# One more step between sign, product, pick, mask and turn of the weights in a top-k attention kernel

## The chip, the cores and the metric

The kernel runs on one core of one Trainium2 chip. The metric is the time of one execution on the device, in microseconds (us). Five runs of the kernel before gave a median of 993.47 us, from 991.87 to 994.64.

## The reference

The inputs are q, k and v of 8 batches, 8 heads, 576 positions and 64 features. Each row of scores keeps its 32 largest entries. The attention output, 4608 tokens of 512 features, then goes through a mixture of 8 experts, each of which takes at most 80 tokens. Shortened to what matters:

```python
scores = scale * np.matmul(q, k.transpose(0, 1, 3, 2))
kth = np.partition(scores, -32, axis=-1)[..., -32:-31]          # 32nd largest of each row
scores = np.where(scores >= kth, scores, -1e9)
attn = np.exp(scores - scores.max(-1, keepdims=True))
attn = attn / (attn.sum(-1, keepdims=True) + 1e-9)
x = np.matmul(attn, v)                                          # -> (4608, 512)
logits = x @ w_gate
expert_idx = np.argmax(logits, axis=1)                          # one expert of 8 for each token
...                                                             # of each expert's tokens the 80 with the largest gate
out[tok_idx] = gate_w[tok_idx, None] * (np.maximum(x[tok_idx] @ w1[e], 0.0) @ w2[e])
```

## The kernel before

The attention part fills some 855 of the 992 us. It works on pairs of heads, `n` = 0 to 31. A pair of heads has 9 *units*: 128 rows of scores against 576 columns each. Four row tiles `t` = 0 to 3 give two units, one for each head (`h` = 0 and 1); the last 64 rows of both heads share one unit (`h` = 2). That makes 288 units, numbered through.

What happens to a unit, and on which engine:

- **front** (L226, L233): TensorE (PE) multiplies q by k into the PSUM tile `sp`, of which there is one; ScalarE (ACT) copies it to the tile `s`. One front makes the scores of two units, or of the one tail unit. It is emitted four steps ahead of their search.
- **parts, search** (L241, L252, L260): VectorE (DVE) takes the 8 largest of six parts, and from these 48 candidates the 24 largest, eight at a time.
- **sign** (L257): ACT writes the sign of (24th largest minus score) and, by the accumulator, how many scores lie above.
- **product** (L263): GpSimd (POOL) multiplies scores and signs into `y`, which has two buffers.
- **max of y** (L265): DVE finds the next 8 candidates below the 24th in `y`.
- **pick** (L268): DVE picks the 32nd largest by the count, as the threshold `thr`.
- **mask** (`below`; L279 or L277): from scores and threshold, on POOL for units of even number and on ACT for odd ones.
- **turn of the weights** (`turn_w`; L315, L320, L322, L324): PE transposes scores and subtracts masks in PSUM, ACT takes the exponential into `wT`. One turn takes the two units of a row tile, or the tail unit.
- **back** (L335): PE multiplies `wT` by v; the row sums come out beside it. Then **over** (L347), the reciprocal on DVE, and **divide** (L358) on ACT, into `xn`.
- After the last row tile of a pair of heads **norm** follows (L367 to L391): store of `xn`, transposes (L201, L375), the gate's logits (L380, L387), and after every eighth pair of heads the gates (L402 to L425). **turn** (L201, L214) transposes q and k of the next pair.

The order is written out by hand, in `run`: under a manual schedule, `step(i)` emits one step of the loop over the units, and every engine works through its own part of that order strictly in sequence. In step i, DVE does the search of unit i and, by a string of letters, pieces of earlier units. The table `back` says by how many units earlier:

```python
back = dict(a=0, b=1, c=1, d=1, e=1, y=2, g=3, h=4, m=4, H=3, M=3)
for c in "GybGcGdGeGGzag" if i % 2 else "GGbghHmMyGcGdGeGza":
```

`G` is one of the six parts, `e` ends with the sign, `y` is the product, `g` the max of y, `h` and `H` are picks, `m` and `M` masks, `z` the reciprocal. Picks and masks come in even steps only, two units at a time. Then follow the turn of the weights of unit i - 4 (if a turn ends there), the divide, the front of unit i + 4, the back of unit i - 5, and in steps without a front the turn of q and k or a piece of norm.

So for each two steps POOL has this order: one mask, two products. DVE has: parts and search of two units, max of y, two more pieces, max of y, pick, pick.

All tiles of the loop come from pools whose buffers rotate: `s` has 5 (each of two units), sign 2, mask 3, the small tiles of the search 4. The three `vb` tiles hold v of three pairs of heads; the loads of q, k and v of pair n + 2 are issued by SyncE (SP) in the step of unit (t = 2, h = 1) of pair n.

After the attention comes the choice of tokens (`route`, DVE alone for the most part) and then the experts, on PE.

Of the kernel before, what the change touches and what calls it, by code (L numbers as in the profile page):

```python
# [9 lines left out]
F32 = mybir.dt.float32  # L10
BF16 = mybir.dt.bfloat16
# [16 lines left out]
def kernel(  # L28
# [12 lines left out]
    B, H, S, D = q.shape  # L41
# [8 lines left out]
    P = 128  # L50
    HP = H // 2
    NP = B * HP
# [11 lines left out]
    NU = NP * UPP  # L64
# [84 lines left out]
    class Attention:  # L149


        def __init__(self, stack, lean):
            self.lean = lean
            pool = lambda name, bufs, **kw: stack.enter_context(tc.tile_pool(name=name, bufs=bufs, **kw))
            self.nat, self.qkp, self.rows = pool("nat", 1), pool("qkp", 2), pool("rows", 2)
            self.small, vpool = pool("small", 4), pool("vpool", 1)
            self.ps_s, self.ps_w, self.ps_c = (pool(n, k, space=PSUM) for n, k in (("ps_s", 1), ("ps_w", 1), ("ps_c", 2)))
            self.qk, self.turned, self.lg = {}, {}, {}
            self.s, self.top, self.cnt, self.y, self.mask, self.w, self.xn = ({} for _ in range(7))
            self.thr, self.z = thr_all, z_all  # L160
            self.odd = set()


            self.vb = []
            for j in range(1 if lean else 3):
                t = vpool.tile([P, NK, 2, D + 1], F32, name=f"vb{j}")
                nc.gpsimd.memset(t[:, :, :, D : D + 1], 1.0)
                nc.gpsimd.memset(t[: P - TL, NF, :, :], 0.0)
                self.vb.append(t)

            self.xT = vpool.tile([P, NK * P], F32, name="xT")
            nc.gpsimd.memset(self.xT[:, S:], 0.0)

        def load(self, n, b, hp):
            one = bass.ds(b, 1)
            tiles = []
            for name, src in (("qn", q), ("kn", k)):
                t = self.nat.tile([P, NK, 2, D], F32, name=name, tag=name)
                for h in range(2):
                    nc.sync.dma_start(  # L180
                        t[:, 0:NF, h, :],
                        src[one, 2 * hp + h, : NF * P, :].rearrange("o (c p) d -> p (o c) d", p=P))
                nc.sync.dma_start(
                    t[0:TL, NF, :, :], src[one, 2 * hp : 2 * hp + 2, NF * P :, :].rearrange("o h p d -> p (o h) d"))
                tiles.append(t)
            t = self.vb[n % len(self.vb)]
            for h in range(2):
                nc.sync.dma_start(
                    t[:, :NF, h, :D], v[one, 2 * hp + h, : NF * P, :].rearrange("o (c p) d -> p (o c) d", p=P))
            nc.sync.dma_start(  # L190
                t[P - TL :, NF, :, :D], v[one, 2 * hp : 2 * hp + 2, NF * P :, :].rearrange("o h p d -> p (o h) d"))
            self.qk[n] = tiles

        def four(self):
            return self.ps_s.tile([P, 4, 512], F32, name="sp", tag="sp")
# [20 lines left out]
        def front(self, n, t):  # L216

            qT, kT = self.turned[n]
            m = P if t < NF else TL
            i = n * UPP + 2 * t  # L220
            ps = self.four()
            for j in range(2):
                for h in range(2):
                    d = slice(D * h, D * h + D)
                    o = ps[:, 2 * h + j, :HS] if t < NF else ps[TL * h : TL * h + TL, j, :HS]
                    nc.tensor.matmul(o, lhsT=qT[d, t * P : t * P + m], rhs=kT[d, j * HS : (j + 1) * HS], start=True, stop=True)  # L226
            g = 2 if t < NF else 1
            s = self.rows.tile([P, 2 * S], F32, name="s", tag="s", bufs=2 if self.lean else 5)
            for h in range(g):
                self.s[i + h] = s[:, h * S : (h + 1) * S]  # L230
            for j in range(0, 2 * g, 2 if i == 0 else 2 * g):
                w = 2 if i == 0 else 2 * g
                nc.scalar.activation(s[:, j * HS : (j + w) * HS].rearrange("p (j c) -> p j c", c=HS), ps[:, j : j + w, :HS],  # L233
                                     Act.Copy, scale=TINY)
# [10 lines left out]
        def search(self, i):  # L245

            s, cand = self.s[i], self.top[i]
            top = self.top[i] = self.small.tile([P, G0 // 8 - 1, 8], F32, name="top", tag="top")
            w9 = self.small.tile([P, 16], F32, name="w9", tag="w9")
            for r in range(G0 // 8):  # L250
                dst = top[:, r, :] if r < G0 // 8 - 1 else w9[:, :8]
                nc.vector.max(out=dst, in_=cand)  # L252
                if r == G0 // 8 - 1:

                    sign = self.rows.tile([P, S], BF16, name="sign", tag="sign")
                    cnt = self.small.tile([P, 1], F32, name="cnt", tag="cnt")
                    nc.scalar.activation(sign, s, Act.Sign, bias=w9[:, 7:8], scale=-1.0, accum_out=cnt)  # L257
                yield
                if r < G0 // 8 - 1:
                    nc.vector.match_replace(out=cand, in_to_replace=dst, in_values=cand, imm_value=LOW)  # L260
                    yield
            y = self.rows.tile([P, S], F32, name="y", tag="y")
            nc.gpsimd.tensor_tensor(out=y, in0=s, in1=sign, op=Alu.mult)  # L263
            yield
            nc.vector.max(out=w9[:, 8:], in_=y)  # L265
            yield
            pick = self.small.tile([P, TOP_K - G0 + 1], F32, name="pick", tag="pick")
            nc.vector.scalar_tensor_tensor(out=pick, in0=past, scalar=cnt, in1=w9[:, 7:], accum_out=self.thr[:, i : i + 1],  # L268
                                           op0=Alu.is_equal, op1=Alu.mult)
            yield  # L270

        def below(self, i):

            self.top.pop(i)
            self.mask[i] = self.rows.tile([P, S], BF16, name="mask", tag="mask", bufs=3)
            if i in self.odd:
                nc.scalar.activation(self.mask[i], self.s[i], Act.Relu, bias=self.thr[:, i : i + 1], scale=-1.0)  # L277
                return
            nc.gpsimd.tensor_scalar(self.mask[i], self.s[i], self.thr[:, i : i + 1], None, op0=Alu.is_lt)  # L279
# [147 lines left out]
        def run(self, slow):  # L427

            units = []
            for n in range(NP):  # L430
                for t in range(NF):
                    units += [(n, t, 0), (n, t, 1)]
                units.append((n, NF, 2))
            self.odd = set(range(1, NU, 2))
            first, second = {}, {}
            later = []
            due = []
            drawn = []
            ready = {}

            def whole(i):

                return 0 <= i < NU and units[i][2] > 0

            def step(i, last):
                if 0 <= i < NU:
                    n, t, h = units[i]
                    if t == 2 and h == 1 and n + 2 < NP:
                        self.load(n + 2, *divmod(n + 2, HP))
                    if t in (1, 3) and h == 0 and slow and n:  # L450
                        slow.pop(0)()
                    if t == 0 and h == 0 and n + 1 < NP:
                        due.append(n + 1)
                    first[i] = self.parts(i)


                back = dict(a=0, b=1, c=1, d=1, e=1, y=2, g=3, h=4, m=4, H=3, M=3)
                for c in "GybGcGdGeGGzag" if i % 2 else "GGbghHmMyGcGdGeGza":
                    if c == "G":
                        if 0 <= i < NU:  # L460
# [15 lines left out]
                drawn.clear()  # L476

                def back():
                    if whole(i - 5):
                        self.back(*units[i - 5][:2])  # L480
                        drawn.append(units[i - 5][:2])


                rest = whole(i - 4) and units[i - 4][2] == 2
                if rest:
                    back()
                if whole(i - 4):
                    self.turn_w(*units[i - 4][:2])
                for u in done:
                    self.divide(*u)  # L490

# [7 lines left out]
                if not rest:  # L499
                    back()  # L500
# [10 lines left out]
                for n, cs in ends:  # L511
                    b, hp = divmod(n, HP)
# [1 line left out]
                    ready[later[-1]] = 0  # L514

            with tc.manual_schedule():
                self.load(0, 0, 0)
                self.load(1, *divmod(1, HP))
                nc.sync.dma_start(wg, moe_w_gate.rearrange("(c p) e -> p c e", p=P))
                self.turn(0)  # L520
                i = -4
                while i < NU + 6 or later:
                    step(i, i >= NU + 5)
                    i += 1
            assert not slow and not due

        def batch(self, b):

            for hp in range(HP):
                self.load(hp, b, hp)  # L530
                self.turn(hp)
                for t in range(NK):
                    self.front(hp, t)
                    i = hp * UPP + 2 * t
# [380 lines left out]
```

## Time and profile before

| | |
|---|---|
| median of 5 runs | 993.47 us (991.87 to 994.64) |
| the profiled execution | 993.92 us; span from its first to its last instruction 992.2 us |
| mean granted TensorE clock | 0.984 |
| from the first POOL mask to the last | 22.36 to 855.63 us |
| choice of tokens and experts | from about 867 us to the end |

| engine | busy us | share of the span |
|---|---|---|
| PE (matmul) | 879.8 | 89% |
| DVE | 804.6 | 81% |
| ACT | 799.2 | 81% |
| POOL | 627.2 | 63% |

How to read it: a group's line names the source line, the engine, the operation and the tiles, then the busy time and the mean of one in ns, then the idle time of the engine just before and what ended it. Matmul ends are modelled, so a busy PE need not be PE at its peak. In the view of the waits the columns are: who waited for whom, us in total, times, the longest in us. In the timeline: start in us, duration in us, engine, line, operation, out<-in, and in brackets the idle time before and what ended it. In the table of stages: the stage, its length, then busy us of PE, PEld (weight loads), DVE, ACT and POOL with the number of instructions in brackets, the granted clock, the DMA engines' share and GB/s.

### The profile page before, as it was taken

What the parts mean: (1) busy time and instruction counts of PE and PEld (TensorE: products, weight loads), DVE (VectorE), ACT (ScalarE), POOL (GpSimd) and SP (SyncE); (2) the same over time, 40 slices, a digit from 0 to 9 for tenths busy, and PEclk for the clock granted to TensorE, in tenths of its full rate; (3) what the DMA queues carried; (4) which work ended last, traced back from release to release, by engine and by line L of the source; (5) the groups of instructions that cost most, each with busy time, mean ns of one, the idle gap of its engine ahead of it and who ended that gap; (6) DMA issues with size and microseconds to landing.
All of it is one profiled execution on the core that took longest, in us unless ns stands there. A gap on an engine that the chain in (4) does not pass through costs nothing.

```text
span 992.2 us, 35679 instructions
## 1 busy us (share of the span) xinstructions
PE 879.8 (89%) x13368; PEld 708.2 (71%) x13368; DVE 804.6 (81%) x4928; ACT 799.2 (81%) x1652; POOL 627.2 (63%) x474
## 2 busy tenths in 40 slices
PE   5899999999989999999899999999899998689896
PEld 3677777777767777777677777777677776678896
DVE  5798989898989898999989898989898989471110
ACT  3899999999989999999899999999899999501110
POOL 3677767676767777777677676767677777402111
PEclk9999999999999999999999999999999999978998
DMA  3444453333323233333111222222222200084920
GB/s 72 101 124 132 127 135 92 92 92 92 93 66 79 79 88 86 88 92 93 42 44 42 47 50 50 51 50 49 49 50 50 49 14 14 16 338 155 376 71 27
DMA packets 167797, 85.76 MB, mean 86 GB/s; under 512 B 117696, under 2 KB 154560, under 8 KB 167616
## 3 DMA queue, kind: packets, MB, share of 16 engines
q1 hardware_dynamic: 166592, 80.78, 29.3%
q0 software_dynamic: 1024, 2.62, 0.9%
q8 instruction: 107, 1.75, 0.7%
q14 instruction: 74, 0.61, 0.2%
HBM read 63.19 MB, written 20.19 MB: 84 GB/s over the span
## 4 chain that ended last, share of the span: by engine, by line
DVE 38%; PE 25%; ACT 21%; POOL 9%; issue 6%; DMA 0%; POOLq 0%; ACTq 0%; DVEq 0%
DVE cand L241 11%; DVE w L265 10%; ACT sign L257 6%; POOL y L263 5%; PE cc L335 5%; ACT wT L324 4%; DVE cand L260 4%; DVE top L252 4%; PE sp L201 4%; POOL mask L279 4%; PE yp L799 4%; PE sp L226 4%; ACT s L233 4%; ACT mask L277 3%; DVE pick L268 3%
## 5 line engine op out<-in xcount | busy, mean ns | idle before, releaser
L241 DVE MAX8 cand<-s 128x8 f32<-128x96 f32 x1728 | 400.9, 246 | 9.3 <-ACT s L233 9.1
L263 POOL TENSOR_TENSOR y<-s,sign 128x576 f32<-128x576 f32 x288 | 365.3, 1280 | 66.4 <-ACT sign L257 66.4
L279 POOL TENSOR_SCALAR mask<-s,thr_all 128x576 bf16<-128x576 f32 x144 | 247.9, 1722 | 178.3 <-DVE pick L268 176.5
L335 PEld LDWEIGHTS cc<-vb,wT 128*64 128x64 f32 x5760 | 183.0, 139 | 114.0 <-ACT wT L324 100.5
L265 DVE MAX8 w<-y 128x8 f32<-128x576 f32 x288 | 216.4, 751 | 46.0 <-POOL y L263 46.0
L335 PE MATMUL cc<-vb,wT 128*64 128x65 f32 x5760 | 205.3, 226 | 42.8 <-ACT wT L324 42.8
L257 ACT ACTIVATE sign<-s,w 128x576 bf16<-128x576 f32 x288 | 225.0, 781 | 6.9 <-POOL y L263 1.9
L226 PE MATMUL sp<-both 64*128 64x288 f32 (+1 forms) x1280 | 203.4, 437 | 17.6 <-ACT part L387 9.6
L233 ACT ACTIVATE s<-sp 128x1152 f32<-128x1152 f32 (+1 forms) x161 | 167.4, 1041 | 12.3 <-PE sp L226 9.9
L315 PE MATMUL ab<-ident,s 128*128 128x128 f32 x1148 | 176.0, 282 | 0.0
L324 ACT ACTIVATE wT<-ab 128x1024 f32<-128x1024 f32 (+1 forms) x159 | 149.0, 937 | 0.0
L226 PEld LDWEIGHTS sp<-both 64*128 64x128 f32 (+1 forms) x1280 | 106.0, 180 | 56.6 <-ACT part L387 11.5
L315 PEld LDWEIGHTS ab<-ident,s 128*128 128x128 f32 x1148 | 127.9, 142 | 11.6 <-issue 0.9
L252 DVE MAX8 top<-cand 128x8 f32<-128x48 f32 x576 | 116.1, 202 | 4.5
L277 ACT ACTIVATE mask<-s,thr_all 128x576 bf16<-128x576 f32 x144 | 112.3, 780 | 6.9 <-DVE pick L268 6.5
L320 PEld LDWEIGHTS <-mask 128*128 128x128 bf16 x1440 | 94.0, 98 | 31.6 <-POOL mask L279 29.1
L260 DVE MATCH_REPLACE8 cand<-top,cand 128x48 f32<-128x48 f32 x576 | 111.0, 193 | 0.0
L358 ACT ACTIVATE xn<-cc,z_all 128x64 f32<-128x64 f32 (+1 forms) x320 | 86.7, 320 | 1.2 <-DVE z_all L347 0.8
L315 PE MATMUL cc<-ident,s 128*128 128x128 f32 x288 | 78.9, 274 | 0.0
L322 ACT ACTIVATE wT<-cc 128x256 f32<-128x256 f32 (+1 forms) x160 | 57.0, 356 | 16.5 <-PE cc L320 15.3
L268 DVE SCALAR_TENSOR_TENSOR pick<-past,cnt,w 128x9 f32<-128x9 f32 x288 | 60.4, 223 | 0.3 <-ACT xn L358 0.3
L257 ACT ACTIVATION_READ_ACCUMULATOR sign<-s,w 128x1 f32 x288 | 58.4, 203 | 0.0
(187 smaller groups left out, 905.9 us busy)
## 6 DMA issues: line engine op xcount, KB each, us to landing
w<-in_moe_w_dram SPq DMA_DIRECT2D x10, 2048.0 KB, 11.8
w<-in_moe_w_dram SPq DMA_DIRECT2D x24, 512.0 KB, 4.6
out_dram<-zero SPq DMA_DIRECT2D x9, 1024.0 KB, 6.5
qn<-in_q_dram SPq DMA_DIRECT2D x64, 128.0 KB, 2.6
kn<-in_k_dram SPq DMA_DIRECT2D x64, 128.0 KB, 2.6
vb<-in_v_dram SPq DMA_DIRECT2D x64, 128.0 KB, 2.7
xd<-xn SPq DMA_DIRECT2D x32, 256.0 KB, 3.9
qn<-in_q_dram SPq DMA_DIRECT2D x32, 32.0 KB, 2.5
```

The lines of the kernel that those rows point to most:

```text
L226: nc.tensor.matmul(o, lhsT=qT[d, t * P : t * P + m], rhs=kT[d, j * HS : (j + 1) * HS], start=True, stop=True)
L233: nc.scalar.activation(s[:, j * HS : (j + w) * HS].rearrange("p (j c) -> p j c", c=HS), ps[:, j : j + w, :HS], Act.Copy, scale=TINY)
L241: nc.vector.max(out=cand[:, j, :], in_=s[:, j * S // NG : (j + 1) * S // NG])
L252: nc.vector.max(out=dst, in_=cand)
L257: nc.scalar.activation(sign, s, Act.Sign, bias=w9[:, 7:8], scale=-1.0, accum_out=cnt)
L260: nc.vector.match_replace(out=cand, in_to_replace=dst, in_values=cand, imm_value=LOW)
L263: nc.gpsimd.tensor_tensor(out=y, in0=s, in1=sign, op=Alu.mult)
L265: nc.vector.max(out=w9[:, 8:], in_=y)
L279: nc.gpsimd.tensor_scalar(self.mask[i], self.s[i], self.thr[:, i : i + 1], None, op0=Alu.is_lt)
L315: nc.tensor.matmul(dst[h][c], lhsT=sc[:, keys[c]], rhs=ident, start=c == 0 or (c == NF and h == 0), stop=False, is_transpose=True, skip_gr ...
L324: nc.scalar.activation(wT[:, : g * NF, :], ab.rearrange("p h c r -> p (h c) r")[:, : g * NF, :], Act.Exp, scale=scale / TINY)
L335: nc.tensor.matmul(cc[r : r + TL, o], lhsT=wT[:, h * NF + c if c < NF else 2 * NF + h, r : r + TL], rhs=vb[:, c, h if t < NF else r // TL, ...
```

## The change

The distances in `back` grow: the product comes three steps after the unit's own step instead of two, the max of y four instead of three, the two picks and masks four and five instead of three and four. The turn of the weights goes from four steps behind to six, the back from five to seven; reciprocal and division stay in the step after the back. As picks and masks come in even steps only, the two units that share such a step are now an odd one (`h`, `m`) and the even one after it (`H`, `M`); before, they were an even one (`h`, `m`) and the odd one after it. The string of letters is the same, and so is which units' masks are made on POOL.

More buffers carry the longer lives: 7 for `s` instead of 5, 3 for sign instead of 2, 4 for mask instead of 3, 7 instead of 4 for the small tiles. The load of v is taken out of `load` and issued two units later. `batch`, a path for other data, loads v in a call of its own.

```diff
-            self.small, vpool = pool("small", 4), pool("vpool", 1)
+            self.small, vpool = pool("small", 7), pool("vpool", 1)
...
+            self.qk[n] = tiles
+
+        def load_v(self, n, b, hp):
+            one = bass.ds(b, 1)
             t = self.vb[n % len(self.vb)]
...
-            s = self.rows.tile([P, 2 * S], F32, name="s", tag="s", bufs=2 if self.lean else 5)
+            s = self.rows.tile([P, 2 * S], F32, name="s", tag="s", bufs=2 if self.lean else 7)
...
-                    sign = self.rows.tile([P, S], BF16, name="sign", tag="sign")
+                    sign = self.rows.tile([P, S], BF16, name="sign", tag="sign", bufs=3)
...
-            self.mask[i] = self.rows.tile([P, S], BF16, name="mask", tag="mask", bufs=3)
+            self.mask[i] = self.rows.tile([P, S], BF16, name="mask", tag="mask", bufs=4)
...
+            LT = 6
...
                     if t == 2 and h == 1 and n + 2 < NP:
                         self.load(n + 2, *divmod(n + 2, HP))
+                    if t == 3 and h == 1 and n + 2 < NP:
+                        self.load_v(n + 2, *divmod(n + 2, HP))
...
-                back = dict(a=0, b=1, c=1, d=1, e=1, y=2, g=3, h=4, m=4, H=3, M=3)
+                back = dict(a=0, b=1, c=1, d=1, e=1, y=3, g=4, h=5, m=5, H=4, M=4)
...
                 def back():
-                    if whole(i - 5):
-                        self.back(*units[i - 5][:2])
-                        drawn.append(units[i - 5][:2])
-                rest = whole(i - 4) and units[i - 4][2] == 2
+                    if whole(i - LT - 1):
+                        self.back(*units[i - LT - 1][:2])
+                        drawn.append(units[i - LT - 1][:2])
+                rest = whole(i - LT) and units[i - LT][2] == 2
                 if rest:
                     back()
-                if whole(i - 4):
-                    self.turn_w(*units[i - 4][:2])
+                if whole(i - LT):
+                    self.turn_w(*units[i - LT][:2])
...
-                while i < NU + 6 or later:
-                    step(i, i >= NU + 5)
+                while i < NU + LT + 3 or later:
+                    step(i, i >= NU + LT + 2)
```

## The prediction

> **What bounds the kernel now.** I read the waits of the whole run first. They say who waits, not what matters.
>
> ```profile
> POOL mask L279 <- DVE pick L268: 176.5, 143, 3.3
> ...
> POOL y L263 <- ACT sign L257: 66.4, 63, 12.3
> ...
> DVE w L265 <- POOL y L263: 46.0, 49, 2.8
> ...
> PEld L320 <- POOL mask L279: 29.1, 35, 2.3
> DVE z_all L347 <- PE cc L335: 27.2, 18, 4.5
> ...
> ACT both L214 <- PE sp L201: 23.1, 31, 2.1
> ```
>
> POOL waits for DVE (mask for pick), DVE for POOL (max of y), POOL for ACT (product for sign). Next I read POOL's timeline in mid-run, from mask to mask.
>
> ```profile
> 300.43 1.72 POOL L279 TENSOR_SCALAR mask<-s,thr_all 128x576 bf16<-128x576 f32 x1 [1.10 <-DVE pick L268]
> 302.12 2.52 POOL L263 TENSOR_TENSOR y<-s,sign 128x576 f32<-128x576 f32 x2
> 305.74 1.72 POOL L279 TENSOR_SCALAR mask<-s,thr_all 128x576 bf16<-128x576 f32 x1 [1.10 <-DVE pick L268]
> ...
> 312.74 1.28 POOL L263 TENSOR_TENSOR y<-s,sign 128x576 f32<-128x576 f32 x1
> 314.66 1.27 POOL L263 TENSOR_TENSOR y<-s,sign 128x576 f32<-128x576 f32 x1 [0.64 <-ACT sign L257]
> 317.03 1.72 POOL L279 TENSOR_SCALAR mask<-s,thr_all 128x576 bf16<-128x576 f32 x1 [1.10 <-DVE pick L268]
> ```
>
> One stretch (two units) lasts 5.31 us, the next but one 5.98, where the second product waits 0.64 for a sign. Counted over the run, from the mask at 38.09 to the last at 855.63 there are 141 stretches in 817.5 us, mean 5.80: 70 of 5.31, 62 above 5.9. DVE's timeline shows how a short one closes.
>
> ```profile
> 304.67 0.76 DVE L265 MAX8 w<-y 128x8 f32<-128x576 f32 x1
> 305.35 0.21 DVE L268 SCALAR_TENSOR_TENSOR pick<-past,cnt,w 128x9 f32<-128x9 f32 x1
> 305.48 0.08 DVE L268 DVE_READ_ACCUMULATOR pick<-past,cnt,w 128x1 f32 x1
> 305.54 0.23 DVE L268 SCALAR_TENSOR_TENSOR pick<-past,cnt,w 128x9 f32<-128x9 f32 x1
> 305.69 0.08 DVE L268 DVE_READ_ACCUMULATOR pick<-past,cnt,w 128x1 f32 x1
> ```
>
> It is a ring: mask 1.69 to the first product, the two products to 304.64, max of y from 304.67, first pick done at 305.56, mask at 305.74. Nothing in it is idle but hand-overs. That the ring binds, and not DVE's load, shows at the end, where DVE has little left to do and the stretch is as long (DVE 3.01 of 5.30):
>
> ```profile
> 317.03:368.78 51.75, 47.42 (x698) 37.63 (x695) 47.98 (x303) 48.95 (x102) 38.01 (x27) 1.00 0.34 88
> ...
> 850.33:855.63 5.30, 4.14 (x88) 3.86 (x84) 3.01 (x13) 3.64 (x10) 4.20 (x3) 1.00 0.01 3
> ```
>
> The first line is the repeating block, two pairs of heads, nine stretches: 51.75 us, of which nine rings are 47.8. ACT is busy 48.95, and of its 2.80 idle 2.35 end on PE: 1.28 before `both` (0.98 and 0.30), 0.20 xT, 0.10 part, 0.66 wT, 0.11 s. So two things bind: the ring in short stretches, ACT with PE in long ones.
>
> **Step 1, the waits for signs.** In the stretch at 305.74 the first product's sign was done 3.1 us before the product began, the second's 0.3 us (sign and accumulator end at 308.34, product at 308.66). That 0.3 is why only the second product waits. One step later (2.65 us, half a stretch), and with the units' parities exchanged, both have about 4 us. From 38.09 on these waits are 46.8 us; I take all of them away. Late next is what ACT itself needs, step 3.
>
> **Step 2, the ring gets a pick longer.** In the order of the changed kernel POOL's mask still belongs to the even unit, but that is now the second pick of the step; in the old order the mask waits for the first. The second accumulator is read 0.21 after the first (305.48, 305.69). Queued behind the mask are both products, and behind those DVE's two maxima, so it is paid in full: 5.31 + 0.21 = 5.52, times 141 is +30 us on the ring. Product to max and pick to mask keep their distances, so the ring isn't opened. Nine rings are 49.7.
>
> **Step 3, ACT.** Its work is the same. The waits for PE before `both`, xT and part stay, for ACT's order around them is the same: 48.95 + 1.58 = 50.5 a block. The waits before wT and s (0.77) I let go: the order puts the tail unit's turn and the logits, which share a step now, into different ones, and no turn waits for a mask of its own step (PE waited 52 us for masks; ACT hides most of it, so I count nothing more). Bounds: 49.7, the ring, if ACT's waits overlap; 51.3 if all 2.35 stay. I take 50.5: 1.25 less a block, 141/9 = 15.7 blocks, **-19.6 us**.
>
> **Step 4, the waits of POOL itself.** In the new order 286 products wait for two engines, an extra wait instruction each: the sign, and POOL's own third instruction back (the buffer of y), long done. Its price can be read from the masks: those that wait for one engine only stand 1.03 idle, the others 1.10.
>
> ```profile
> 22.36 1.74 POOL L279 TENSOR_SCALAR mask<-s,thr_all 128x576 bf16<-128x576 f32 x1 [1.03 <-DVE pick L268]
> ```
>
> So 0.07 when POOL waits for it, nothing while POOL works on the instruction ahead; products follow back to back and their signs are done, so I take 0. Bounds 0 to 0.2 each (0.16 from pick's end to mask, and 0.04 of overlap lost).
>
> The Trainium skill speaks against the change here: "Perfetto Trace Analysis", section Identifying Dependency Chains, says that an instruction that waits on several engines may get an extra semaphore instruction before it, and "Advanced Engine Details and Errata", section Network/Comms, puts reading a semaphore at 50 to 100 ns. By these, as an estimate, 286 products would pay 14 to 29 us, and the sum below would come to between -6 and +9 instead of -20.
>
> **Step 5, start, gates, end.** At the start DVE waits 2.83 and 1.12 us for products held by signs; bounds -6 to 0, I take -3. Three times the gates stretch three stretches by some 2.8 us together; that is DVE work and stays. At the end POOL makes y of the last unit after the last mask, not before it: mask to product 1.69, product 1.28, max to pick 0.68, pick and hand-over 0.39, ACT's mask 0.7 comes before the exponential that began 2.11 after the mask: 4.74 - 2.11 = **+2.6**.
>
> Costing nothing: more buffers (old rotation had no waits of its own), the load of v two steps later (used two pairs of heads, some 50 us, afterwards; behind it on SP are weights, zeros and stores that nobody awaits there), and fewer double waits on DVE's picks.
>
> **Sum.** Against this execution's own 993.92 (span 992.2 and 1.7 around it; 0.45 above the median): -19.6 - 3 + 2.6 = -20.0, so **973.9 us**.
>
> **Rivals.**
> - *The ring alone sets the pace.* ACT catches up in short stretches, with 4 us of reserve. 141 x 5.52 + 8.4 for gates = 786.7 against 817.5: -31, with start and end 963. For: ACT's 5.0 to 5.2 busy in short stretches. Against: the 1.28 before `both`, ACT in order.
> - *The waits move.* DVE's reciprocal stands one step behind the back, with 1.2 to 1.6 us of reserve in short stretches, and waits already (27.2 us, one of 1.30 in the block). If ACT keeps its 51.3 and DVE now waits there, the gain is 0 to 7 us: 987 to 994.
> - *Slower: POOL pays for the extra wait.* Place: both products of the ring. At 0.2 each the ring is 5.92, 141 x 5.92 + 8.4 = 843 against 817.5: +26, 1019. It decides from (5.80 - 5.52)/2 = 0.14 a product. For: the ring has no slack and the wait for a mask shows a price. Against: POOL starts instructions 0.03 to 0.04 before the record of the one ahead ends, so it looks ahead.
> - *The change doesn't do what it says:* the string of letters keeps picks in even steps, so even units' pick and mask are no later than before; that is step 2, priced.
>
> **Chances.** Forecast (967 to 987) 0.53; ring alone (955 to 967) 0.12; waits move 0.17, of which 0.08 within 0.2% (2 us, about what a measurement of this kernel can tell from no change), 0.07 faster and 0.02 slower; POOL's price 0.18. Faster 0.53 + 0.12 + 0.07 = 0.72, same 0.08, slower 0.20. The range 960 to 998 leaves out half of the ring's case and most of POOL's, some 0.2.
>
> **What would show it.** Step 1: no wait of y for sign after 38 us. Step 2: short stretches of 5.5, the mask released by the second pick. Step 3: blocks of 50.5 with ACT at 97%. Step 4: products back to back; gaps of 0.1 or more between mask and product prove me wrong. Step 5: 4.7 from the last POOL mask to the exponential. If short stretches are still 5.3, the ring was not what bound them; if L347's waits grow beyond 40 us, the second rival holds.

## The result, and the profile after

The changed kernel takes **996.35 us** (median of 31 runs, 994.63 to 998.22) against 993.59 for the kernel before (53 runs in the same sessions). The ratio is 1.0024, 95% interval 1.0018 to 1.0030. Where 20 us of gain were forecast, it is slower by 2.4 us on the mean: little, but the interval lies above 1. The profiled execution took 995.53 us, with a span of 993.8.

POOL's timeline after, in mid-run:

```profile
388.57 2.52 POOL L266 TENSOR_TENSOR y<-s,sign 128x576 f32<-128x576 f32 x2
392.40 1.72 POOL L282 TENSOR_SCALAR mask<-s,thr_all 128x576 bf16<-128x576 f32 x1 [1.31 <-DVE pick L271]
394.09 2.52 POOL L266 TENSOR_TENSOR y<-s,sign 128x576 f32<-128x576 f32 x2
399.98 1.72 POOL L282 TENSOR_SCALAR mask<-s,thr_all 128x576 bf16<-128x576 f32 x1 [3.37 <-DVE cand L244]
```

A *stretch* is the time from one POOL mask to the next (two units), a *block* nine stretches (two pairs of heads), after which the pattern repeats. The two products run back to back without a gap: the sign waits are gone. The mask's idle time in a short stretch is 1.31 or 1.25 instead of 1.10, the longer ring. But nearly every block (14 of 16) now has one stretch of over 7 us like the last, 7.58 us, in which POOL waits 3.37 for a threshold. The page names DVE's maximum of a part (`cand`), merely the instruction that DVE finished last. DVE's own timeline shows where it lost the time:

```profile
393.64 0.17 DVE L350 RECIPROCAL z_all<-cc 128x2 f32<-128x2 f32 x1 [0.36 <-PE cc L338]
...
396.52 0.17 DVE L350 RECIPROCAL z_all<-cc 128x1 f32<-128x1 f32 x1 [1.07 <-PE cc L338]
...
397.86 0.75 DVE L268 MAX8 w<-y 128x8 f32<-128x576 f32 x1
398.53 0.21 DVE L271 SCALAR_TENSOR_TENSOR pick<-past,cnt,w 128x9 f32<-128x9 f32 x1
```

The reciprocals wait for TensorE's back, and the maxima and the picks stand behind them. The waits of the whole run say the same:

```profile
POOL mask L282 <- DVE pick L271: 68.3, 47, 3.3
DVE z_all L350 <- PE cc L338: 48.0, 63, 4.2
ACT s L236 <- PE sp L229: 29.6, 36, 2.4
PEld sp L383 <- ACT s L236: 19.7, 30, 1.0
POOL y L266 <- ACT sign L260: 13.7, 2, 12.5
DVE w L268 <- POOL y L266: 7.8, 6, 3.1
```

POOL's wait for signs fell from 66.4 to 13.7 us (both that are left lie before 31 us), and DVE's for products from 46.0 to 7.8. DVE's wait for the back rose from 27.2 to 48.0, and ACT's for the scores of a front from 9.9 to 29.6. The block is longer, in the table of stages:

```profile
364.50:416.83 52.33, 47.30 (x693) 37.58 (x692) 47.95 (x301) 48.39 (x103) 37.91 (x28) 1.00 0.32 87
```

It takes 52.33 us instead of 51.75, with less busy time of ACT (48.39 against 48.95) and more idle time: 3.94 instead of 2.80.

By parts of the profiled execution, in us:

| part | forecast | measured | from |
|---|---|---|---|
| start, to the third POOL mask, from which the forecast counts its 141 stretches | -3 | -4.18 | 38.09, 33.91 |
| third to last POOL mask | -19.6 | +1.15 | 817.54, 818.69 |
| last mask to the gates' last exponential | +2.6 | +3.95 | 11.71, 15.66 |
| choice of tokens and experts | 0 | +0.69 | 124.86, 125.55 |
| sum | -20.0 | +1.61 | |

The second row holds nearly all of the forecast's error. It is itself a sum of two things. There are 141 stretches or 15.7 blocks in it, and 15.7 times 0.58 is +9.1; the other -7.9 come for the most part from the gates. Four blocks with one of the gates in them took 210.6 before, 3.6 more than four times 51.74; after, 208.9 to 210.9 by where the count starts, 209.7 on average, 0.4 more than four times 52.33, for the block behind the gates takes only 50.0 to 50.4. A pace that gates on DVE hardly lengthen any more is not likely to be DVE's or the ring's.

### The profile page after: what moved, and what is told of

Its sections match the earlier page's. It is cut to its first block, busy times and chain, and to the rows that moved or that the text cites. A ratio compares the mean times of both kernels' runs of the same rounds, so it can differ in the third digit from the quotient of the medians.

```text
span 993.8 us, 35784 instructions
## 1 busy us (share of the span) xinstructions
PE 876.0 (88%) x13368; PEld 706.7 (71%) x13368; DVE 813.0 (82%) x4928; ACT 789.5 (79%) x1652; POOL 625.2 (63%) x474
## 4 chain that ended last, share of the span: by engine, by line
PE 32%; ACT 25%; DVE 25%; issue 10%; POOL 7%; DMA 1%; POOLq 0%; DVEq 0%; SPq 0%; ACTq 0%
PE cc L338 11%; DVE w L268 8%; ACT wT L327 7%; DVE cand L244 6%; ACT sign L260 6%; ACT mask L280 5%; POOL y L266 5%; PE sp L229 4%; PE yp L807 4%; PE sp L204 3%; DVE cand L263 3%; ACT s L236 3%; PE ab L318 2%; ACT wT L325 2%; POOL mask L282 2%
## 5 line engine op out<-in xcount | busy, mean ns | idle before, releaser
L266 POOL TENSOR_TENSOR y<-s,sign 128x576 f32<-128x576 f32 x288 | 363.2, 1282 | 13.7 <-ACT sign L260 13.7
L236 ACT ACTIVATE s<-sp 128x1152 f32<-128x1152 f32 (+1 forms) x161 | 167.8, 1043 | 30.3 <-PE sp L229 29.6
L350 DVE RECIPROCAL z_all<-cc 128x2 f32<-128x2 f32 (+1 forms) x160 | 26.0, 162 | 49.7 <-PE cc L338 48.0
```

## The experiments

Theory A says that the longer ring and the wait of the reciprocals set the block; theory B that the pair of TensorE and ACT, which hand one another the PSUM tiles (`sp` for scores and small pieces, `ab` and `cc` for the turn of the weights and the back), set it by themselves in the order that the change gives them. Blocks below are the nine stretches that repeat in mid-run, away from the gates.

**1. The ring.** First the changed kernel with POOL's masks on the odd units, which are released by the first pick (a ring of 5.31 again), then the kernel before with the same edit; there it is the second pick that releases them (5.52).

```diff
-            self.odd = set(range(1, NU, 2))
+            self.odd = set(range(0, NU, 2))
```

> The changed kernel, with one thing other: POOL makes the masks of the odd units and ACT those of the even ones, so POOL's mask is again released by the first pick of a step, as before the change. Theory A (the longer ring sets the short stretches, the reciprocal's wait for the back the long one of each block): short stretches 5.31 instead of 5.47 to 5.52, the long one of 7.57 stays, 10 to 17 us less than the changed kernel's 996.4, so 979 to 986. Theory B (the chain of PE and ACT alone sets the block, and the ring only fits itself in): blocks stay at 52.3, within 3 us of 996.4.

995.88 us, ratio 1.0013 (0.9997 to 1.0028). Short stretches are 5.31 to 5.33, the block is 52.29: the ring got 1.9 a block shorter and the block did not move. The reciprocals' wait took it:

```profile
DVE z_all L350 <- PE cc L338: 63.8, 68, 4.2
```

> The kernel before, with one thing other: POOL makes the masks of the odd units and ACT those of the even ones, so that POOL's mask waits for the second pick of a step. This is step 2 of the prediction alone. Theory A: the 70 short stretches go from 5.31 to 5.5, +14 us, and the long ones, which are not set by the ring, stay: 1003 to 1008. If DVE's load and not the ring sets 5.31: no change, 991 to 996. If the ring stands in every stretch: +30, 1023.

992.91 us, ratio 0.9985 (0.9972 to 0.9998), blocks of 51.84 to 51.96 instead of 51.74. A ring longer by 0.21 in every stretch (74 short stretches of 5.5 instead of 70 of 5.3) cost the whole run nothing; the waits for signs fell from 66.4 to 36.5 us instead. The ring of the forecast did not set the pace, before or after.

**2. The reciprocals.** The changed kernel without them; the row sums are taken as 32.

```diff
-    nc.gpsimd.memset(z_all, 1.0)
+    nc.gpsimd.memset(z_all, 1.0 / TOP_K)
...
-            nc.vector.reciprocal(z, z if self.lean else sums)
+            if self.lean:
+                nc.vector.reciprocal(z, z)
```

> The changed kernel without the reciprocals on DVE: the division takes a constant 1/32 instead, so DVE never waits for PE's back. Theory A: the 48 us of DVE's waits for the back go, the long stretch of 7.57 falls to 5.5 to 6, blocks to between the ring's 49.7 and 51: 20 to 40 us less than 996.4. Theory B: ACT and PE still need 51 to 52 a block, DVE is held elsewhere (sign, scores, masks), 10 us less at most.

The block is 52.35, with the same stretch of 7.58 in it; DVE now waits 39.3 us for products. The wait at the reciprocal is a symptom: theory A falls. The time, 1000.18 us (ratio 1.0054, 1.0037 to 1.0071), is longer for the most part behind the attention: 128.9 us from the gates' last exponential to the end instead of 125.6, which no run here explains.

**3. TensorE and ACT alone.** The search is left out, in the changed kernel and in the one before.

```diff
-                nc.vector.max(out=cand[:, j, :], in_=s[:, j * S // NG : (j + 1) * S // NG])
                 yield
...
-                    nc.scalar.activation(sign, s, Act.Sign, bias=w9[:, 7:8], scale=-1.0, accum_out=cnt)
+                    nc.scalar.activation(sign, s, Act.Sign, bias=thr_all[:, i : i + 1], scale=-1.0, accum_out=cnt)
...
-            nc.gpsimd.tensor_tensor(out=y, in0=s, in1=sign, op=Alu.mult)
```

> The changed kernel with the search left out: DVE's maxima, replacements and picks and POOL's products are not computed, sign and mask take a constant threshold (the output is that of another threshold). TensorE and ACT do exactly their old work in their old order, and wait only for each other, for POOL's masks and for the reciprocals. Theory B (the pair of TensorE and ACT sets the pace by itself): nine stretches of the mask take 52 to 52.5 us, as in the changed kernel, no block is longer where the gates lie, and the time is 985 to 997. Theory C (a loop through DVE and POOL sets the pace, the pair is able to do better): 49.7 to 51, and 960 to 978.

> The kernel before with the same left out. Theory B: nine stretches take 51.7 to 52.4 us, and the time stays within 10 us of before; if the places of the turns matter to the pair, this one is 0.3 to 0.6 a block shorter than the changed kernel treated the same way. Theory C: 49 to 51, with no difference between the two orders, 955 to 975.

The whole times, 3351 and 3327 us, say nothing: thresholds of zero send the kernel through its branch for other data as well, which I had overlooked in the expectation. The loop ahead of it can be read. The stages of one block, the changed order first:

```profile
400.00:452.40 52.40, 47.29 (x693) 37.58 (x692) 2.10 (x12) 48.38 (x102) 15.49 (x9) 1.00 0.33 87
```

```profile
400.00:451.08 51.08, 47.02 (x692) 37.61 (x690) 1.93 (x12) 48.52 (x102) 15.49 (x10) 1.00 0.35 90
```

With DVE nearly idle (2.1 us) the changed order still takes 52.40, within 0.1 of the full kernel (52.33). **The pair of TensorE and ACT sets the changed kernel's pace**, and neither of them is full. The order before takes 51.08: the change costs the pair 1.3 us a block. The search added 0.66 to that before (51.74), and the gates.

**4. Later turns alone.** The kernel before with the turn of the weights six and the back seven steps behind, product and picks at their old distances (buffers and loads as in the change). Against the changed kernel, which has `LT = 6` already, this is one line:

```diff
-                back = dict(a=0, b=1, c=1, d=1, e=1, y=3, g=4, h=5, m=5, H=4, M=4)
+                back = dict(a=0, b=1, c=1, d=1, e=1, y=2, g=3, h=4, m=4, H=3, M=3)
```

> The kernel before with the second half of the change alone: the turn of the weights six steps behind and the back seven, with the changed kernel's buffers and loads, but sign, product, pick and mask at the distances of before. No turn waits for a fresh mask, turns fall on the same steps as in the changed kernel. Theory A: the ring is 5.31 and the signs' waits (46.8 us) stay; if the new places of turns, fronts and logits cost something by themselves, blocks grow to 52 to 53 with waits of the reciprocal: 993 to 1010. Theory C (the new places are harmless and earlier masks help PE and ACT): 980 to 992.

1048.42 us (ratio 1.055, 1.0521 to 1.0579), block 55.60. That is no answer: the masks of the odd units, which ACT makes, live two steps longer here than in the changed kernel, four buffers were too few, and ACT's masks waited 34.2 us for TensorE's last reads. With six mask buffers:

> The kernel before with only the turn of the weights and the back two steps later, and six mask buffers, so that no mask waits for one; product, max, picks and masks at their old distances, so a ring of 5.31 and signs as late as before. Theory B with the places of the turns as the cause of the longer block: the repeating block is 52.3 us as in the changed kernel, the time 995 to 998. If the later picks were the cause instead: a block of 51.75 and 992 to 995. If the waits for signs had kept the pace at before's places: 51.75 too.

1004.28 us (ratio 1.0091, 1.0065 to 1.0118), block 52.66. Of the distances, the turns' and backs' alone make the block longer, and now the loss is booked where it was before the change:

```profile
POOL y L266 <- ACT sign L260: 77.9, 73, 12.3
...
DVE z_all L350 <- PE cc L338: 14.5, 15, 4.2
```

**5. Other distances of turn and front.** What the pair sees of the change is how many steps lie between the turn of a unit and the front emitted in the same step: eight before (turn 4 behind, front 4 ahead), ten after (6 and 4). Nine was tried with `LT = 5` in the changed kernel:

> The changed kernel with the turn of the weights five steps behind instead of six, the back six instead of seven, so that the turns fall into the steps without a front. Theory B: the order of TensorE and ACT is what matters, so the block changes, to 51.5 or less if turn and front in different steps let the two work side by side, to 53 or more if TensorE now waits for ACT's mask of the same step; the waits for signs stay away either way. Theory C: the block is the same 52.3 as long as picks and products stay where they are.

1063.26 us (ratio 1.0696, 1.0669 to 1.0724), blocks mostly of 55.8 to 57.5. Fronts now share their steps with backs instead of turns, and wait for ACT's copies of the small pieces out of the one PSUM tile `sp`:

```profile
PEld sp L229 <- ACT xT L378: 61.5, 30, 2.3
...
PEld sp L229 <- ACT both L217: 42.0, 31, 1.6
```

So one step less between turn and front costs over 60 us here, which none of the forecast's terms could have shown. Then eight again, with the later products and picks kept; the edit is against the changed kernel:

```diff
-            LT = 6
+            LT = 5
...
-                    if t == 0 and h == 0 and n + 1 < NP:
+                    if t == 1 and h == 0 and n + 1 < NP:
...
-                f = i + 4 if i not in (0, 1) else i + 3
+                f = i + 3
...
-                i = -4
+                i = -3
```

> The changed kernel with its later products, picks and masks, but with TensorE and ACT in the order of the kernel before: the turn of the weights five steps behind and the front three ahead, eight steps apart as before (the changed kernel has ten), q and k turned one step later so that they keep their place too. If the distance of turn and front is what made the block longer: no waits for signs, short stretches of 5.5, blocks of 50.4 to 51.3 (the pair alone took 51.08), no wait of ACT for the front's scores, and 970 to 985 us, faster than both kernels. If the longer ring or the later picks were the cause after all: 52.3 and about 996. If DVE is now short of scores, made one step later: new waits of the six parts for ACT's scores and 985 to 1000.

**980.64 us**, ratio 0.9860 (0.9838 to 0.9881), faster than both kernels. The stages of a block:

```profile
353.20:404.39 51.19, 47.59 (x692) 37.50 (x691) 48.04 (x300) 48.45 (x102) 37.87 (x27) 1.00 0.34 90
```

No wait for signs after 25 us, short stretches of 5.46 to 5.52, blocks of 51.22, and 206.3 for four of them with gates. The later products and picks do help, by 12.7 us, once the order of TensorE and ACT is as it was. The change's larger buffers and later load of v are in this run too, so they are not what made the block longer.

> The same with POOL's masks for the units of odd number, so that the mask is released by the first pick and the ring is 5.31 instead of 5.52. If TensorE and ACT set the pace in the run before: no difference within 2 us, the same blocks. If the ring of 5.52 (49.7 a block) had become the bound there: 1 to 2 us less a block, 15 to 30 us faster.

976.35 us, ratio 0.9825 (0.9807 to 0.9842), with the same blocks (51.25) though short stretches are 5.32: the ring does not bind here either. It is 4.3 us faster all the same, more than the 2 expected. The profiled runs, whose spans differ by 8.2, show where: by the picks, 1.2 are won in the first ten units, 2.1 little by little, and 1.0 with the last unit; 2.3 more come from there to the gates' last exponential, and 1.7 behind it. In 277 units between the first ten and the last, a ring that is 0.21 shorter per two units would have won 29.

> The first of this set with the search left out, as in the two runs without search: a constant threshold, TensorE and ACT with their old work in the order of the kernel before. If the order sets the pair's pace: 51.1 a block, as in the kernel before without search, against 52.4 in the changed order. The whole time is not comparable, since the branch for other data follows.

Without search this order takes 51.21 a block, against 51.08 and 52.40: the pair's pace, and the full kernels' 51.22 and 51.25 are that pace to within 0.1. This run and the one with 52.40 have the same work and the same buffers; they differ only in where the turns and backs, the fronts and the turn of q and k stand.

> The changed kernel with its turn six steps behind, and the front two steps ahead instead of four: eight steps apart again, by moving the front alone. If the distance counts: the waits of ACT for the front's scores and of TensorE's logits for ACT go as in the run with five and three. But scores are there only one stretch ahead of the search, so DVE's parts may wait for ACT: 975 to 1000, with blocks of 50.5 to 52.6.

1018.29 us (ratio 1.0256, 1.0235 to 1.0278), worse than the worst that I expected, with blocks around 54. It can't tell: scores come too late for DVE, a new wait that hides what the pair would do.

```profile
DVE cand L244 <- ACT s L236: 77.3, 83, 7.7
```

**6. Which place costs it.** After the change, one step holds the turn of the tail unit and the front of the next pair's first row tile, and the step behind it the tail's back and the gate's logits. ACT's and TensorE's timelines of the changed kernel there:

```profile
368.01 0.28 ACT L325 ACTIVATE wT<-cc 128x128 f32<-128x128 f32 x1
368.19 0.59 ACT L327 ACTIVATE wT<-ab 128x512 f32<-128x512 f32 x1
369.42 1.13 ACT L236 ACTIVATE s<-sp 128x1152 f32<-128x1152 f32 x1 [0.64 <-PE sp L229]
```

```profile
367.75 0.39 PE L323 MATMUL ab<-minus,mask 128*128 128x128 bf16 x4
368.07 1.24 PE L229 MATMUL sp<-both 64*128 64x288 f32 x8
369.24 0.80 PE L338 MATMUL cc<-vb,wT 128*64 128x65 f32 x20
370.60 0.76 PE L383 MATMUL sp<-wg,xT 128*64 128x8 f32 x20 [0.56 <-ACT s L236]
```

ACT's exponentials of a tail are short (0.77 from start to end), the front takes 1.24, so ACT stands still for 0.64. Then TensorE has only the tail's back (0.80) while ACT copies 1.13 out of `sp`, so the logits, which need `sp`, wait 0.56. Both happen twice a block. Before, the logits stood behind the tail's turn; ACT's next copy followed its exponentials without a wait that the timeline shows:

```profile
340.49 0.28 ACT L322 ACTIVATE wT<-cc 128x128 f32<-128x128 f32 x1
340.72 0.60 ACT L324 ACTIVATE wT<-ab 128x512 f32<-128x512 f32 x1
341.41 0.19 ACT L387 COPY part<-sp 128x40 f32<-128x40 f32 x1
```

The next run moves norm's pieces alone; the condition picks the steps for them, by the number of the step modulo 9.

```diff
-                    if ready[g] and busy and not last:
+                    if ready[g] and (i % 9 not in (6, 8) if i < NU else busy) and not last:
```

> The changed kernel with two pieces of norm in other steps: the transposes of xn in the step of the tail's back (where the logits were), the logits two steps later; turns, backs and fronts stay where they are. If the logits' place costs the block: TensorE's wait of the logits for ACT's copy goes, blocks of 51.2 to 51.6, 980 to 986 us. If the front behind the tail's turn costs it: ACT still waits some 0.6 us twice a block for its scores, TensorE's wait moves to whatever piece stands behind the tail's back, blocks of 51.9 to 52.4, 988 to 997 us.

985.77 us (ratio 0.9924, 0.9910 to 0.9939) with blocks of 51.86. Between the two, the time in the first range and the block just below the second: ACT still waits for the front, 0.64 and 0.58 a block, and the transposes of xn wait in the logits' place (ACT, then TensorE):

```profile
366.12 1.13 ACT L236 ACTIVATE s<-sp 128x1152 f32<-128x1152 f32 x1 [0.64 <-PE sp L229]
```

```profile
367.31 0.86 PE L204 MATMUL sp<-ident,xn 128*128 128x128 f32 x5 [0.56 <-ACT s L236]
```

But 0.47 of the 1.1 that the old order saves a block is had by moving the small pieces. The rest, by subtraction, goes with the place of turns and fronts. ACT's waits in the blocks show the same two parts: in the changed kernel 1.22 for the front's scores and 1.10 before the exponentials; with the small pieces moved 1.22 and 0.58; in the order of before with later products and picks (980.64 us) 0.11 and 0.91.

> The faster kernel (turn five steps behind, front three ahead, POOL's mask released by the first pick) with the logits and the transposes of xn in steps in which a turn or a back of two units stands beside them. If small pieces matter only where they stand behind a short back: no change within 2 us. If they matter everywhere: some 0.2 us a block, 2 to 5 us faster.

The condition here names steps 0 and 7. **962.82 us**, ratio 0.9689 (0.9676 to 0.9703), the fastest of all; blocks of 50.16 most often (49.4 to 50.6), 1.1 less than without it, where I had expected 0.2. In the order of the kernel before, the tail's front waits for the copy of the logits (0.29 and 0.54 in its block); this is gone, and 0.24 and 0.28 of a wait of the logits stand in its place. ACT's waits before the exponentials fall too, from 0.91 to 0.18 a block. How these add up to 1.1 is not shown.

The runs of the mechanism, in a table of blocks (and medians):

| | order of TensorE and ACT as before | as changed |
|---|---|---|
| without search | 51.08, 51.21 | 52.40 |
| products and picks as before | 51.74 (993.6) | 52.66 (1004.3) |
| products and picks later | 51.22 (980.6) | 52.33 (996.4) |

## Why the prediction was wrong, by its own steps

**Step 1 (signs)** was right: no wait of a product for a sign after 38 us (the last is at 30.28). But what it is worth is not the sum of these waits, 46.8 us, nor the 19.6 that step 3 made of it. With the order held, later products and picks brought 12.7 us in all.

**Step 2 (ring)** was right in its size, 5.31 to 5.52, released by the second pick, and wrong in what it meant. That the ring binds was argued from a stretch at the end where DVE has little to do; two runs with the other ring, and a third in the better order, left the blocks within 0.2 of where they were.

**Step 3 (ACT) is the step that failed.** It made the block of ACT's busy time and a part of its waits for TensorE, 48.95 + 1.58 = 50.5, on two grounds: that ACT's order around the waits that stay is the same, and that the waits before wT and s (0.77 a block) go, because the tail's turn and the logits fall into different steps. The waits that should stay did, 1.50 of 1.58 (`both` 1.30, xT 0.20). Those let go came to 2.32 a block, three times what they were: for the front's scores 1.22 instead of 0.11, before the exponentials 1.10 instead of 0.66.

```profile
ACT s L236 <- PE sp L229: 1.2, 2, 0.6
ACT wT L325 <- PE cc L323: 1.1, 2, 0.6
```

With 48.39 of busy time and 3.94 of idle time that is the measured 52.33. The step did not ask which front falls into the tail's step instead; that front is what ACT now waits for. And it took what was left over as slack: the pair alone, with the search left out, takes 51.08 in the old order and 52.40 in the new. With 51.2 in place of 50.5 the same sum would have come to about -9, and with 52.4 to about +10; the gates, which the pair covers, are the main thing that brought it down to +1.6. So the change ended near nothing by two effects that nearly cancel, +9.1 in the blocks and some -8 mostly at the gates, and no step foresaw either: that the measured time is so near to before is luck of the sum. The step also read 52 us of TensorE's waits for masks out of two rows (29.1 for weight loads, 23.1 for matmuls) that count the same time twice; they are 29.1 together, and no term rested on them.

**Step 4 (POOL's extra waits)** was right: of 288 products only the two at 16.29 and 30.28 us have a gap above 0.02 ahead of them, though 286 have the extra wait instruction. So the instruction that the Trainium skill speaks of ("Perfetto Trace Analysis", Identifying Dependency Chains) is there, but the estimate of 14 to 29 us, for which the time to read a semaphore ("Advanced Engine Details and Errata", Network/Comms) was taken as its price, did not come: here it cost nothing where POOL had work ahead of it.

**Step 5 (start, gates, end).** The start, up to the third mask, brought 4.18 instead of 3, within its bounds. The gates were said to stay, as DVE's work; what they add to four blocks fell from 3.6 to 0.4. The end cost 3.95 instead of 2.6: from the last POOL mask to the exponential it is 5.84, not 4.74, since TensorE's subtraction of the mask between ACT's mask (856.72) and the exponential (858.44) was left out of the chain.

**The rivals.** "The waits move" came nearest: the wait at the reciprocals grew to 48.0, beyond the 40 us named. But it kept ACT at 51.3, and so ended at 987 to 994; the pair's pace itself got worse, and the reciprocal only shows it. "The ring alone" and POOL's price are out.

## What to carry to other kernels

Here two engines hand each other PSUM tiles, some of them with a single buffer, and their joint pace came from the order of their work; neither busy times nor the waits of the other engines showed it. Cutting the other engines' work out and timing the pair alone did. A change of distances in a software pipeline, a loop whose engines work on different units at the same time, also changes which pieces meet in one step; write out the steps of one period before and after, look for a short piece beside a long one, and only then add up what the removed waits were worth. Slack given to an engine that is not the bound came back here as a wait under another name: of DVE for the back (27.2 to 48.0 us), and without reciprocals for products (39.3 us).

## What was not expected of the hardware

- TensorE busy 47.3 and ACT 48.4 of 52.4 us, at a granted clock of 1.00, and still nothing but the two of them binding: in the run without search, 3.9 of ACT's 4.0 us of idle time in a block are waits for TensorE, and 4.7 of TensorE's 5.1 are waits for ACT (waits of 0.15 us and more).
- Moving two small pieces (0.8 us each on TensorE, 0.2 and 0.66 on ACT) took 1.1 us off a block and 13.5 us off the run.
